# Softmax scaling split between ScalarE and VectorE, and the second 64-token score unit moved behind two other groups of products

## The chip, the cores and the metric

The kernel runs on one core of one Trainium2 chip. The metric is the device time of one execution in microseconds; the median of three runs counts. The engines of the core work in parallel, each through its own queue in order: TensorE (PE in the rows, its weight loads PEld), VectorE (DVE), ScalarE (ACT), GpSimd (POOL) and the queue that issues the transfers (SP).

## The reference

Two layers follow each other, for 8 batches of 576 tokens. The first is a causal retention over 8 heads of 64: `((q kᵀ / 8) * gamma_h^(i-j) for j <= i) v`. Its output, 512 wide, is the input `x` of the second, a mixture of 4 experts:

```python
logits = x @ w_gate                      # 4 experts, the best 2 chosen per token
w = softmax over the chosen 2
for e in range(4):
    a = softmax(causal((x @ wq[e]) @ (x @ wk[e]).T / 8))
    out += (e chosen) * w_e * (a @ (x @ wv[e]) @ wo[e])
```

What the change touches is the softmax `a`: the exponentials have to be divided by their sum and multiplied by the token's weight for the expert before they meet the values.

## The kernel before, in words

Tokens are cut into 36 tiles of 128 (9 for each pair of batches; the ninth holds the last 64 tokens of both), three tiles to a group, 12 groups. The main loop (line 514) runs over stages `j` = 0 to 14 and in each over three rounds `i` = 0, 1, 2. Round `i` of stage `j` does, in this order of issue:

- the retention of tile `n = 3j + i`: `qk(n+1)` (scores of the next tile), `old(n)` (product with the state), later `own(n)` (product inside the chunk) and `state(n+1)`;
- between `old` and `own`, the scores of the experts for one unit of group `j - 2` (`scores`, lines 330 to 382). A unit is one tile, or, for the ninth tile, two units of 64 tokens each ("tail" units). Both tail units fall into the third round. That happens in stages 4, 7, 10 and 13; I call the third rounds of stages 4, 7 and 10 the **tail rounds**. In stage 13 there is no retention left;
- the softmax of the unit: VectorE reads the scores from PSUM and finds the maxima (line 368, for tails 373), ScalarE exponentiates and sums (line 379), VectorE makes the reciprocal times the weight (lines 391 to 393) and scales (line 398). `normal(u)` holds lines 391 to 398;
- in between, as `work`, the projections of group `j - 1` (`pj` line 250 in one round, `pv` line 274 in the others) and the output product of group `j - 3` (`po` line 470);
- `split` (line 210 on ScalarE, 211 on GpSimd), which makes the two-part form of the retention's result.

After the three rounds the stage transposes the scaled weights on TensorE (`pt`, line 416), copies them out of PSUM on VectorE and ScalarE in turn (lines 420 and 422), works out the gate (lines 300 to 319), and multiplies with the values (`ys`, lines 442 to 449).

A unit's `p32` tile holds its pieces side by side: four experts for a whole unit, two pieces for a tail unit (expert pairs lie on the two halves of the partitions). A whole unit at place t = 0 to 3 of its batch has pieces 64 + 128t, 64 + 128t, 128 + 128t and 128 + 128t wide; a tail unit has two of 576. The second piece (`e` = 1) is scaled in two parts, the last 64 columns of it being written behind the first piece. So a whole unit has five scaling instructions (four at t = 0) and a tail unit three.

Engines, order and waits are fixed by the order of issue: each engine takes its instructions in program order, and an instruction waits only for the regions that it reads or writes. All PSUM tiles come from one pool of eight banks (`bank`, tag "b"); a bank is handed out again in the order in which the banks were given back, so each product on TensorE waits for the engine that empties the bank which is next in that order: `pv`, `pj` and `own` may wait for line 368 or 373, `own` for the copy of `qk` (line 144) or of `po` (line 473), `state` for the copy of `old` (line 169).

Of the kernel before, what the change touches and what calls it, by code (L numbers as in the profile page):

```python
# [11 lines left out]
AF = mybir.ActivationFunctionType  # L12
OP = mybir.AluOpType
# [18 lines left out]
def chunks(n):  # L32
    pair, i = divmod(n, 9)
    if i == 8:
        return [(2 * pair, 8), (2 * pair + 1, 8)]
    return [(2 * pair + i // 4, 2 * (i % 4)), (2 * pair + i // 4, 2 * (i % 4) + 1)]


def units(g):
    out = []  # L40
    for n in range(3 * g, 3 * g + 3):
        out += [(n, 0), (n, 1)] if n % 9 == 8 else [(n, None)]
    return out
# [3 lines left out]
def kernel(ctx: ExitStack, tc: tile.TileContext, xf, vkf, wraw, gi_d, con_d, out):  # L47
# [8 lines left out]
    act = nc.scalar.activation  # L56
    v = nc.vector
    gp = nc.gpsimd

    def bank(shape, name):  # L60
        return pool.tile(shape, F32, name=name, tag="b")
# [24 lines left out]
    def load(n, w):  # L86
        if n >= NT:
            return
        if w == 0:
            X[n] = x = ld.tile([128, 2, 4, 128], F32, name="x", tag="x")  # L90
            nc.sync.dma_start(x, xf[n])
        else:
            VK[n] = vk = ld.tile([128, 2, 2, 4, D], F32, name="vk", tag="vk", bufs=4)
            nc.sync.dma_start(vk, vkf[n])
# [6 lines left out]
    def decay(n, e=None):  # L101
        if n >= NT:
            return
        vv = VK[n][:, :, 0]
        k = chunks(n)[0][1]
        gm = gam[:, 8:9] if k == 8 else gam[:, k:k + 2]
        (e or gp).tensor_mul(vv, vv, gm.unsqueeze(3).to_broadcast([128, 2, 4, D]))  # L107

    def state(n):
        if n >= NT or n % 9 == 8:  # L110
            return
        vk = VK[n]
        ps = [bank([128, 2, 2, D], "st") for r in range(2)]
        for s in range(2):
            for u in range(2):
                for r in range(2):
                    for g in range(2):
                        h = 2 * g + u
                        mm(ps[r][HALF[g], s, u], vk[HALF[r], s, 1, h], vk[HALF[r], s, 0, h], start=True, stop=True)  # L119
        for s, (b, k) in enumerate(chunks(n)):  # L120
            last = k == 7
            S_[b, k] = w = sa.tile([128, 2, 2, D], F32, name="s7" if last else "s", tag="s7" if last else "s",
                                   bufs=3 if last else 4)
            for r in range(2):
                if k == 0:
                    v.tensor_copy(w[:, r], ps[r][:, s])
                else:
                    v.tensor_add(w[:, r], ps[r][:, s], S_[b, k - 1][:, r])
# [194 lines left out]
    def place(u):  # L323
        n, s = u
        if s is None:
            t = n % 9 % 4
            return t, SLOT[t], 4
        return 4, 3 + s, 2

    def scores(u):  # L330
        m, tail = u
        t, slot, n = place(u)
        g, l0 = m // 3, 128 * (m % 3)
        q, k = Q[g, "q"], K[g // 3]
        t0 = 128 * t
        ws = [t0 + 64, t0 + 64, t0 + 128, t0 + 128]
        if tail is None:
            kb = 512 * (m % 9 // 4)
            if t < 2:
                two = [bank([128, 2, t0 + 128], "ss") for z in range(2)]  # L340
                ps = [two[e % 2][:, e // 2, :ws[e]] for e in range(n)]
            else:
                ps = [bank([128, ws[e]], "ss") for e in range(n)]
            for s in range(2):
                for p in range(2):
                    for z in range(2):
                        e = 2 * s + z
                        mm(ps[e][HALF[p]], q[p][HALF[z], l0 + 64 * s:l0 + 64 * s + 64], k[p][HALF[z], kb:kb + ws[e]],  # L348
                           start=True, stop=True)
        else:  # L350
            kb = [slice(512 * tail, 512 * tail + 512), slice(1024 + 64 * tail, 1088 + 64 * tail)]
            ps = [[bank([128, 512 if j == 0 else 64], "ss") for j in range(2)] for z in range(2)]
            for j in range(2):
                for p in range(2):
                    for z in range(2):
                        mm(ps[z][j][HALF[p]], q[p][HALF[z], l0 + 64 * tail:l0 + 64 * tail + 64], k[p][HALF[z], kb[j]],
                           start=True, stop=True)
        p32 = sb.tile([128, PSZ[slot]], F32, name="p32", tag=f"p32{slot}")
        p32 = p32[:, :n * (t0 + 128)].rearrange("p (n w) -> p n w", n=n)
        sm = sb.tile([128, 2, E], F32, name="sm", tag="sm", bufs=6)  # L360
        nm = sb.tile([128, E], F32, name="nm", tag="nm", bufs=6)
        SS[u] = (p32, sm, ws)

        def soft():
            bias = []
            for e in range(n):
                if tail is None:
                    v.tensor_tensor_reduce(p32[:, e, :ws[e]], ps[e], mask[:, 576 - ws[e]:], -1.0, BIG, OP.add, OP.min,  # L368
                                           nm[:, e:e + 1])
                    bias.append(nm[:, e:e + 1])  # L370
                else:
                    for j, c in enumerate((slice(0, 512), slice(512, 576))):
                        v.tensor_tensor_reduce(p32[:, e, c], ps[e][j], mask[:, c],  # L373
                                               -1.0, nm[:, 2 * e:2 * e + 1] if j else BIG, OP.add, OP.min,
                                               nm[:, 2 * e + j:2 * e + j + 1])
                    bias.append(nm[:, 2 * e + 1:2 * e + 2])
            yield
            for e in range(n):
                act(p32[:, e, :ws[e]], p32[:, e, :ws[e]], AF.Exp, bias=bias[e], scale=-1.0, accum_out=sm[:, 0, e:e + 1])  # L379
                yield  # L380

        return soft()

    def normal(u):
        m, tail = u
        t, slot, n = place(u)
        t0 = 128 * t
        p32, sm, ws = SS[u]
        wt = WT[m // 3]
        rs = sm[:, 1, :n]  # L390
        v.tensor_scalar(sm[:, 0, :n], sm[:, 0, :n], 1e-9, None, op0=OP.add)
        v.reciprocal(rs, sm[:, 0, :n])
        v.tensor_mul(rs, rs, wt[:, m % 3].rearrange("p s z -> p (s z)") if tail is None else wt[:, 2, tail])  # L393
        for e in range(n):
            parts = [(e, 0, ws[e])] if e != 1 else [(1, 0, t0)] * (t > 0) + [(0, t0 + 64, 64)]
            for f_, c0, cw in parts:
                i0 = c0 if f_ == e else t0
                v.tensor_scalar(p32[:, f_, c0:c0 + cw], p32[:, e, i0:i0 + cw], rs[:, e:e + 1], None, op0=OP.mult)  # L398

    FLIP = [0]  # L400

# [75 lines left out]
    def run(*gs):  # L477
        for g in gs:
            for _ in g:
                pass  # L480
# [33 lines left out]
    for j in range(NG + 3):  # L514
        us = units(j - 2) if 0 <= j - 2 < NG else []
        for i in range(3):
            n = 3 * j + i
            if n < 2:
                decay(n + 1, v)
            if n != 2:  # L520
                qk(n + 1)
            old(n)
            work = stage(j, i)
            here = us[i:i + 1] if i < 2 else us[2:]
            soft = [scores(u) for u in here]
            for sc in soft:
                next(sc)
            own(n)
            if n == 2:
                qk(3)  # L530
            state(n + 1)
            load(n + 3, 0)
            load(n + 4, 1)
            if n == 0:
                fetch("o")
            scale(n, v if n < 3 else None)
            if 2 < n + 2 and i < 2:
                decay(n + 2)
            for u, sc in zip(here, soft):
                for _ in sc:  # L540
                    next(work, None)
                normal(u)
            split(n)
            if 0 < n + 1 < 5:
                table(n + 1)
            if i == 2:
                decay(n + 2)
            if n == 1:
                weights("k")
            if n == 2:  # L550
                weights("q", gp)
                weights("v")
            if n == 5:
                weights("o")
            run(work)
        for u in us:
            run(turn(u))
        if 0 <= j - 1 < NG:
            gate(j - 1)
        for u in us:  # L560
            values(u, u[0] == NT - 1)
# [56 lines left out]
```

## Time and profile before

| | |
|---|---|
| median of three runs | 477.23 us (476.7 to 477.42) |
| profiled execution, its own time | 473.82 us |
| its span, first to last instruction | 471.4 us |
| mean granted TensorE clock | 0.964 |
| PE busy | 434.9 us (92%) |
| DVE busy | 335.5 us (71%) |
| ACT busy | 260.3 us (55%) |
| POOL busy | 217.8 us (46%) |

The profile is of one execution; its own time is its span and 2.4 us around it, and it is 0.7% under the median of the runs. Times in the rows are microseconds from the start of the span. In a timeline row, the first number is the start, the second how long it (or the merged group, with x and its count) took, and brackets show how long the engine had been idle just before and which instruction ended that.

### The profile page before, as it was taken

How to read it: one execution, taken by the hardware profiler on the slowest of the kernel's cores; microseconds unless marked ns; L12 is line 12 of the kernel's file. 1: busy time of each engine (PE TensorE's matmuls, PEld its weight loads, DVE VectorE, ACT ScalarE, POOL GpSimd, SP SyncE). 2: the span in 40 equal slices, each digit the busy share in tenths (PEclk: the TensorE clock that was granted, in tenths of full speed). 3: DMA queues.
4: the chain of work that ended last, by engine and by line, in shares of the span. 5: the costliest groups of instructions: out<-in, count | busy, mean ns of one | idle time of the engine just before them, and what ended most of it. 6: DMA issues, size and time to landing. Idle time of an engine off the chain costs nothing.

```text
span 471.4 us, 18746 instructions
## 1 busy us (share of the span) xinstructions
PE 434.9 (92%) x7876; PEld 396.5 (84%) x7876; DVE 335.5 (71%) x1141; ACT 260.3 (55%) x762; POOL 217.8 (46%) x272
## 2 busy tenths in 40 slices
PE   6679888999989999999989999999999999999786
PEld 4578778889869998889969998889969999898476
DVE  2462777886898668886898678886898567665490
ACT  2545464664655564664665575664664466564552
POOL 4576573663653464563653365463653254202001
PEclk8679889999999999999999999999998999999979
DMA  8953432251351053242361063242250011010101
GB/s 279 405 204 117 155 99 83 92 182 68 110 186 46 26 198 119 90 159 92 93 202 48 1 214 125 91 160 91 92 203 3 3 36 36 1 68 2 68 1 69
DMA packets 18900, 50.90 MB, mean 108 GB/s; under 512 B 2304, under 2 KB 9088, under 8 KB 18816
## 3 DMA queue, kind: packets, MB, share of 16 engines
q1 hardware_dynamic: 18816, 49.71, 30.8%
q8 instruction: 62, 1.02, 0.9%
q14 instruction: 22, 0.18, 0.1%
HBM read 40.26 MB, written 9.44 MB: 105 GB/s over the span
## 4 chain that ended last, share of the span: by engine, by line
PE 77%; DVE 11%; ACT 4%; issue 4%; POOL 2%; DMA 1%; SPq 0%; ACTq 0%; POOLq 0%; DVEq 0%
PE pj L250 22%; PE pv L274 10%; PE pt L416 9%; PE po L470 7%; PE ys L442 6%; PE ss L348 5%; DVE p L398 5%; PE own L183 4%; PE qk L141 3%; PE st L119 3%; PE old L166 2%; DVE sm L393 2%; ACT p L379 2%; PE ys L449 2%; PE ys L446 2%
## 5 line engine op out<-in xcount | busy, mean ns | idle before, releaser
L379 ACT ACTIVATE p<-p,nm 128x128 f32<-128x128 f32 (+8 forms) x144 | 79.6, 554 | 41.8 <-DVE nm L368 27.2
L398 DVE TENSOR_SCALAR p<-p,sm 128x64 f32<-128x64 f32 (+8 forms) x176 | 81.6, 527 | 1.4
L460 POOL CAST yh<-y 128x256 fp32r<-128x256 f32 (+1 forms) x38 | 14.4, 379 | 124.5 <-ACT y L459 124.5
L147 POOL TENSOR_SCALAR_AFFINE_SELECT p<-p 64x512 f32<-64x512 f32 x72 | 49.1, 683 | 32.5 <-ACT p L144 29.9
L368 DVE CUSTOM_DVE_ANT_0 p<-ss,mask 128x128 f32<-128x128 f32 (+7 forms) x128 | 51.0, 453 | 17.2 <-PE ss L348 16.4
L200 POOL TENSOR_TENSOR x<-x,gi 128x512 f32<-128x512 f32 x29 | 37.4, 1290 | 47.7 <-DVE x L188 47.4
L211 POOL TENSOR_TENSOR xl<-x,xh 128x512 fp32r<-128x512 f32 x36 | 46.7, 1298 | 23.2 <-ACT xh L210 23.1
L420 DVE COPY pth<-pt 128x512 f32<-128x512 f32 (+2 forms) x52 | 31.3, 618 | 28.2 <-PE pt L416 27.8
L416 PE MATMUL pt<-con,p 128*128 128x128 f32 x360 | 43.8, 282 | 4.1 <-DVE nm L373 4.1
L416 PEld LDWEIGHTS pt<-con,p 128*128 128x128 f32 x360 | 42.5, 147 | 4.6 <-DVE nm L373 4.2
L183 PEld LDWEIGHTS own<-p,vk 64*64 64x64 f32 x1152 | 27.3, 144 | 21.9 <-issue 11.7
L183 PE MATMUL own<-p,vk 64*64 64x64 f32 x1152 | 28.8, 230 | 14.3 <-DVE nm L373 4.8
L442 PE MATMUL ys<-pth,vn 128*64 128x128 f32 (+1 forms) x640 | 39.2, 254 | 0.0
L348 PE MATMUL ss<-k,q 64*64 64x512 f32 (+7 forms) x512 | 38.9, 410 | 0.2
L107 POOL TENSOR_TENSOR vk<-vk,con 128x512 f32<-128x512 f32 x33 | 36.2, 1098 | 0.1
L422 ACT ACTIVATE pth<-pt 128x512 f32<-128x512 f32 (+2 forms) x52 | 27.3, 540 | 9.3 <-PE pt L416 9.3
L210 ACT ACTIVATE xh<-x 128x512 fp32r<-128x512 f32 x36 | 22.5, 626 | 17.3 <-POOL x L200 9.6
L473 ACT ACTIVATE ot<-po 128x384 f32<-128x384 f32 x48 | 23.4, 489 | 14.2 <-PE po L470 13.7
L442 PEld LDWEIGHTS ys<-pth,vn 128*64 128x64 f32 x640 | 29.0, 138 | 1.3 <-issue 1.2
L144 ACT ACTIVATE p<-qk 128x256 f32<-128x256 f32 x72 | 23.6, 379 | 11.9 <-PE qk L141 9.7
L141 PEld LDWEIGHTS qk<-x 64*64 64x64 f32 x1152 | 22.4, 145 | 9.2 <-issue 8.2
L119 PE MATMUL st<-vk 64*64 64x64 f32 x1024 | 26.1, 235 | 4.3 <-DVE vk L107 2.7
(93 smaller groups left out, 1051.3 us busy)
## 6 DMA issues: line engine op xcount, KB each, us to landing
x<-xf SPq DMA_DIRECT2D x36, 512.0 KB, 3.8
vk<-vkf SPq DMA_DIRECT2D x36, 512.0 KB, 4.7
out<-ot SPq DMA_DIRECT2D x48, 192.0 KB, 1.9
raw<-wraw SPq DMA_DIRECT2D x4, 512.0 KB, 8.8
gi<-gi SPq DMA_DIRECT2D x1, 256.0 KB, 8.2
con<-con SPq DMA_DIRECT2D x1, 110.0 KB, 3.3
mask<-con SPq DMA_DIRECT2D x1, 32.0 KB, 7.9
rg<-wraw SPq DMA_DIRECT2D x1, 8.0 KB, 8.8
```

The source lines that it names most:

```text
L119: mm(ps[r][HALF[g], s, u], vk[HALF[r], s, 1, h], vk[HALF[r], s, 0, h], start=True, stop=True)
L147: gp.affine_select(w, w, pattern=[[0, 8], [1, 64]], base=0, channel_multiplier=-1, compare_op=OP.is_ge, fill=0.0)
L183: mm(ps[r][HALF[u], g, i], vk[HALF[r], s, 0, 2 * g + u], p[HALF[r], g, s, u], start=True, stop=True)
L211: (e or gp).tensor_sub(xl[:, :, l0:l0 + 128], x32, f(xh[:, :, l0:l0 + 128]))
L250: mm(ps, ww[:, kc, p * 128:(p + 1) * 128], xx[:, kc, c], start=(i == 0), stop=(i == 11))
L274: mm(ps, xx[:, kc, l0:l0 + 128], ww[:, kc], start=(i == 0), stop=(i == 11))
L348: mm(ps[e][HALF[p]], q[p][HALF[z], l0 + 64 * s:l0 + 64 * s + 64], k[p][HALF[z], kb:kb + ws[e]], start=True, stop=True)
L368: v.tensor_tensor_reduce(p32[:, e, :ws[e]], ps[e], mask[:, 576 - ws[e]:], -1.0, BIG, OP.add, OP.min, nm[:, e:e + 1])
L379: act(p32[:, e, :ws[e]], p32[:, e, :ws[e]], AF.Exp, bias=bias[e], scale=-1.0, accum_out=sm[:, 0, e:e + 1])
L398: v.tensor_scalar(p32[:, f_, c0:c0 + cw], p32[:, e, i0:i0 + cw], rs[:, e:e + 1], None, op0=OP.mult)
L416: nc.tensor.transpose(pt[:, i], src, ident)
L442: mm(py[HALF[z], p], VN[n0 + j][:, e * D:(e + 1) * D], src, start=(j == 0), stop=False)
```

## The change

Two edits. In `normal`, the pieces with even `e` (the first and the third of a whole unit, the first of a tail unit) are scaled by a ScalarE copy with a per-token scale instead of a VectorE multiplication; the pieces with odd `e` stay where they are. In the main loop, only the first unit of a round has its scores issued ahead of `own` and `state`; a second one, which exists only in rounds with two tail units, has its scores and its VectorE maxima issued behind them.

```diff
             for f_, c0, cw in parts:
                 i0 = c0 if f_ == e else t0
-                v.tensor_scalar(p32[:, f_, c0:c0 + cw], p32[:, e, i0:i0 + cw], rs[:, e:e + 1], None, op0=OP.mult)
+                if e % 2 == 0:
+                    act(p32[:, f_, c0:c0 + cw], p32[:, e, i0:i0 + cw], AF.Copy, scale=rs[:, e:e + 1])
+                else:
+                    v.tensor_scalar(p32[:, f_, c0:c0 + cw], p32[:, e, i0:i0 + cw], rs[:, e:e + 1], None, op0=OP.mult)
...
-            soft = [scores(u) for u in here]
+            soft = [scores(u) for u in here[:1]]
             for sc in soft:
                 next(sc)
             own(n)
             if n == 2:
                 qk(3)
             state(n + 1)
+            for u in here[1:]:
+                soft.append(scores(u))
+                next(soft[-1])
```

## Rows read from the trace of the kernel before

**Rows 1.** The page: busy time, share of the span and instructions of each engine.
```profile
PE 434.9 (92%) x7876; PEld 396.5 (84%) x7876; DVE 335.5 (71%) x1141; ACT 260.3 (55%) x762; POOL 217.8 (46%) x272
```

**Rows 2.** The page: the chain that ended last, by engine.
```profile
PE 77%; DVE 11%; ACT 4%; issue 4%; POOL 2%; DMA 1%; SPq 0%; ACTq 0%; POOLq 0%; DVEq 0%
```

**Rows 3.** TensorE's waits: who waited for whom, total us, times, longest.
```profile
PE own L183 <- DVE nm L373: 4.8, 3, 1.6
PE pt L416 <- DVE nm L373: 4.1, 1, 4.1
PE own L183 <- DVE lg L289: 3.0, 3, 1.7
PE pj L250 <- DVE nm L368: 2.4, 3, 1.2
```

**Rows 4.** Timeline, VectorE, around the tail round of stage 7.
```profile
242.36 0.77 DVE L391 TENSOR_SCALAR sm<-sm 128x4 f32<-128x4 f32 x1 [0.25 <-ACT p L379]
243.38 1.22 DVE L393 TENSOR_TENSOR sm<-sm,wt 128x4 f32<-128x4 f32 x1
244.63 2.50 DVE L398 TENSOR_SCALAR p<-p,sm 128x448 f32<-128x448 f32 x5
```

**Rows 5.** The same stretch, GpSimd.
```profile
242.06 1.04 POOL L107 TENSOR_TENSOR vk<-vk,con 128x512 f32<-128x512 f32 x1
243.30 1.27 POOL L211 TENSOR_TENSOR xl<-x,xh 128x512 fp32r<-128x512 f32 x1 [0.20 <-ACT xh L210]
```

**Rows 6.** The same stretch, ScalarE.
```profile
242.14 0.20 ACT L379 ACTIVATION_READ_ACCUMULATOR p<-p,nm 128x1 f32 x1
242.60 0.63 ACT L210 ACTIVATE xh<-x 128x512 fp32r<-128x512 f32 x1
243.20 0.49 ACT L473 ACTIVATE ot<-po 128x384 f32<-128x384 f32 x1
243.82 0.66 ACT L144 ACTIVATE p<-qk 128x256 f32<-128x256 f32 x2
```

**Rows 7.** The same stretch, TensorE.
```profile
244.07 2.18 PE L356 MATMUL ss<-k,q 64*64 64x512 f32 x32
247.88 1.12 PE L183 MATMUL own<-p,vk 64*64 64x64 f32 x32 [1.63 <-DVE nm L373]
249.88 0.98 PE L250 MATMUL pj<-xh,whk 128*128 128x384 f32 x4
```

**Rows 8.** Timeline, VectorE, stage 13, where GpSimd is idle.
```profile
441.36 1.47 DVE L398 TENSOR_SCALAR p<-p,sm 128x320 f32<-128x320 f32 x5
447.62 1.74 DVE L398 TENSOR_SCALAR p<-p,sm 128x448 f32<-128x448 f32 x5
```

**Rows 9.** ScalarE by line and form: count, busy us, mean ns, idle before.
```profile
L379 ACT ACTIVATE p<-p,nm 128x512 f32<-128x512 f32 x16 | 11.4, 713 | 0.0
L379 ACT ACTIVATE p<-p,nm 128x128 f32<-128x128 f32 x16 | 6.2, 389 | 0.0
L99 ACT ACTIVATE gi<-gi,con 128x128 f32<-128x128 f32 x12 | 3.8, 386 | 0.0
```

**Rows 10.** Timeline, TensorE, second round of stage 2.
```profile
64.51 0.68 PE L183 MATMUL own<-p,vk 64*64 64x64 f32 x28 [1.72 <-DVE lg L289]
```

**Rows 11.** Timeline, ScalarE and TensorE, first and second round of stage 9.
```profile
308.90 0.49 ACT L473 ACTIVATE ot<-po 128x384 f32<-128x384 f32 x1 [0.56 <-PE po L470]
311.28 0.62 PE L183 MATMUL own<-p,vk 64*64 64x64 f32 x26 [0.89 <-DVE nm L368]
```

**Rows 12.** Timeline, ScalarE and TensorE, end of stage 13.
```profile
452.53 0.78 ACT L379 ACTIVATE p<-p,nm 128x576 f32<-128x576 f32 x1 [0.18 <-DVE nm L373]
454.36 1.82 ACT L422 ACTIVATE pth<-pt 128x512 f32<-128x512 f32 x4
457.49 0.66 PE L442 MATMUL ys<-pth,vn 128*64 128x128 f32 x8
```

**Rows 13.** Stretch, PE, PEld, DVE, ACT, POOL busy (count), granted clock, DMA share, GB/s.
```profile
356.00:358.00 2.00, 2.00 (x25) 1.93 (x15) 1.71 (x10) 1.34 (x4) 0.00 (x0) 0.56 0.03 8
```

## The prediction

> **What bounds the kernel now.** I read the page's busy times first, then the chain that ended last, then who waits for whom on TensorE, then the four engines side by side where TensorE waits. TensorE is busy 92% of the span [rows 1] and makes 77% of the last chain [rows 2]; VectorE has 11% of that chain and ScalarE 4%. So time is lost or won only where TensorE stands still. The list of its waits is short [rows 3]: 4.8 us in three pieces of 1.6 before `own`, for the maxima of the tail units; 3.0 us before `own`, for a VectorE copy behind the scaling; 2.4 us before `pj`; and 4.1 us once, at the end, before the transposes. All four end with VectorE, and in all of them VectorE is late because it was scaling the unit before. That is the most that the change can take away: some 14 us, less what takes its place.
>
> **The change, part by part.** *What moves.* 32 whole units give up two scalings each and 8 tail units one: 72 of 176.
>
> *VectorE's saving.* Where GpSimd is idle, the five scalings of a unit at t = 2 (1408 columns) took 1.47 us and at t = 3 (1920 columns) 1.74 us [rows 8]. The difference gives 0.53 ns a column, and what is left 0.15 us an instruction. First and third piece are 960 columns at t = 3, 704, 448 and 192 at t = 2, 1 and 0: saved 0.81, 0.67, 0.54, 0.40 us, and 0.46 for a tail. In all 8 x 2.42 + 8 x 0.46 = 23 us.
>
> *ScalarE's cost.* The trace has a scaled copy of another table, 128 wide: 12 in 3.8 us, 0.32 apart [rows 9]. The slope comes from exponentials 512 and 128 wide, 713 and 389 ns [rows 9]: 0.84 ns a column. So a unit costs ScalarE 1.23, 1.02, 0.80, 0.59 us (t = 3 to 0) and a tail 0.70, in all 35 us, on an engine with 211 us idle [rows 1]. Bounds from the rows: below, the columns alone (0.81 us at t = 3); above, full durations that don't overlap (1.37 us). I take 1.23, from the one row that is the same operation.
>
> *The new wait.* ScalarE takes its queue in order. Behind a unit's last exponential it now waits for lines 391 to 393. Behind that wait stand `xh` (line 210), the copies of `pv` and `po`, then those of `qk` and `old` of the next round, whose banks TensorE needs. What that wait costs: in stage 7 the last sum was ready at 242.34 [rows 6], line 391 ended at 243.13 and line 393 only at 244.60 [rows 4]. Both ended within 0.1 us of a GpSimd instruction: L107 at 243.10, L211 at 244.57 [rows 5]. But L211 needs `xh`, and `xh` will stand behind the scalings. So line 393, no longer beside L211, ends near 243.55, and the wait is about 1.2 us instead of 2.3; the VectorE scalings, 2.50 us beside GpSimd [rows 4], take 0.9 for three pieces.
>
> *The tail rounds (stages 4, 7, 10).* Worked through for stage 7. VectorE is free at 243.55 + 0.9 + some slack = 244.6 instead of 247.13 [rows 4], so it no longer is what is late. ScalarE: scalings 243.7 to 244.9, `xh` to 245.45, the `po` copy ends at 245.95 (before: 243.69), the `qk` copies at 246.25 and 246.5 (before: 244.48) [rows 6]. TensorE: the first tail's scores began at 244.07 and the two tails took 2.18 us together [rows 7]; the last bank of the first one is that of the `po` copy, so it finishes at 246.15, about 0.9 us late. `own` then needs the `qk` banks (246.55, just behind), ends near 246.95, `state` near 247.6, the second tail's scores, whose banks VectorE has emptied, near 248.7, and `pj` starts near 248.75 instead of 249.88 [rows 7]. Gain 1.1 us a round, 3.3 in all. The second edit does part of this: with it, `own` waits for `qk`'s banks and not for the first tail's maxima. Inside the round the exponentials of the second tail come later, but 8 us of `pj` hide that.
>
> *Stage 2.* The 1.72 us before `own` [rows 10] end when the last VectorE copy behind the scaling is done. Two waits of line 393 for GpSimd go, ScalarE adds its scalings ahead of that copy: I get 63.85 instead of 64.51, 0.7 us. The longest of the three `pj` waits, 1.2 us [rows 3], is in the third round of the same stage; the `qk` and `old` copies, then late, leave 0.5 us of gain. Together 1.2.
>
> *Where the wait only changes its name.* In stage 9 (and 3 and 6) `own` waited 0.89 us [rows 11]. The `po` copy that frees its first bank ended at 309.39 [rows 11]; behind 1.2 us of scalings and what they wait for it ends near 311.2, so `own` starts at the same 311.2. The same in the third rounds of stages 5, 8 and 11 to 0.1 us. I count these as 0.
>
> *The end (stage 13).* Here nothing covers. The order on ScalarE is: both exponentials of tail A, scaling of A, both of tail B, scaling of B, seven copies of transposes. The scaling of A waits for lines 391 to 393, which stand on VectorE behind the maxima of B. B's first exponential could start at 452.53 [rows 12], when the maximum of its first piece was there; the second's takes 0.9 more, 453.4. VectorE arrives 1.4 us earlier (0.67 + 0.81 less scaling in the two units before), so its maxima end at 452.05, lines 391 to 393 at 452.65, A is scaled by 453.4, so the first exponential of B starts at 453.4 instead of 452.53, and the copies start at 456.6 instead of 454.36 [rows 12]. The last transposes wait for the fifth of these, so `ys` starts near 459.1 instead of 457.49 [rows 12]: a loss of 1.6 us. TensorE, which stands idle 4.1 us ahead of the transposes today [rows 3], will then do so between them, so I add 0.4 for a lower clock.
>
> *Clock.* After the stall in stage 10 the granted clock was 0.56 for two microseconds and more [rows 13], the lower of its two levels, 1.2 GHz, for most of that time; 0.44 x 2 = 0.9 us. The stalls get shorter; I count half, 0.5 us.
>
> *Transfers.* Output transfers leave with the `po` copies, up to 2 us later, and the loads queue behind them on SP; they run two to three tiles ahead, so I count nothing. Were that cover gone, it would be these 2 us a round.
>
> **Sum.** -3.3 - 1.2 - 0.5 + 2.0 = -3.0 us: 470.8 against the profiled execution's 473.82. The same difference from the median of the runs: 474.2.
>
> **The rivals.**
> *A: ScalarE becomes what is late.* In 12 rounds (one each in stages 2, 3, 5, 6, 8 and 9, two each in 4, 7 and 10) I have TensorE start within 0.2 us of the moment when a ScalarE copy frees its bank. Each 0.1 us more per unit costs 1.2 us, so 0.25 us more than assumed uses up the gain. Price with 0.5 (the upper bound, 0.14, and a line 393 as late as before in a third of the rounds): 12 x 0.5 = 6, sum +3.0, 480.2. For it: the per-unit cost of 1.23 against 0.81 saved. Against it: ScalarE idles 211 us in all [rows 1], and where that idling stands ahead of a copy that has to wait for TensorE anyway, it catches up and the lateness doesn't add up from round to round. The Trainium skill, page "ScalarE: Activation LUTs", section "Rules for kernel authors", would keep a multiplication on VectorE because it is faster there per element. By that rule, 35 us bought with 23 would be a loss wherever ScalarE is on the chain; the rows agree on the prices, not on where the chain runs.
> *B: the wait changes its name in the tail rounds too.* Then -3.3 goes to 0: sum about +0.3, 477.5. For it: that is what I expect in stages 3, 5, 6, 8 and 9. Against it: in the tail rounds 2.5 us of VectorE lateness go.
> *C: more is won.* The stall at the end doesn't come, since ScalarE overlaps better than I count, and all clock drops go: -3.3 - 1.2 - 1.5 = -6.0, 471.2.
> *D: pieces of one `p32` tile on two engines wait for each other.* They touch different columns, so I don't expect it; it would act as A.
>
> **Chances.** My forecast 0.52, A with D 0.18, B 0.17, C 0.13. Two runs of this kernel can't be told apart below about 0.2%, 0.95 us. Faster by more: 0.62 (nearly all of the forecast, C, a little of B); same 0.17 (B); slower 0.21 (A, the rest). The range 470.6 to 478.2 holds C, forecast and B, and leaves out A's end. The forecast's own range is 472.2 to 476.2.
>
> **What would show it.** Tail rounds: no `own` wait for line 373, and `pj` about 1.1 us earlier after `qk`. Line 393 near 0.16 us instead of up to 1.22. New TensorE waits for ScalarE lines 473 and 144. In stage 13, exponentials of the second tail separated by a ScalarE wait for line 393, and `ys` later. I am wrong if TensorE's waits for ScalarE add up to more than 4 us, or if the tail rounds are no shorter.

## The result, and the profile after

The changed kernel took 471.62 us (median of 4 runs, 470.5 to 472.33) against 476.97 us of the kernel before on the same chip (4 runs): ratio 0.9885, 95% interval 0.9863 to 0.9907, or 5.4 us faster. Measured again beside the experiments it took 471.52 us against 476.07: ratio 0.9909 (0.9881 to 0.9936), 4.6 us. The forecast was 474.2, 3.0 us faster. The two profiled executions differ by 3.3 us (470.5 and 473.82) and their spans by 2.9 us (468.5 and 471.4).

The page after, against [rows 1, 2]: VectorE is busy 62.5 us less and has 4% of the last chain instead of 11%; ScalarE is busy 26 us more and has 7% of it instead of 4%.

```profile
PE 436.8 (93%) x7876; PEld 397.9 (85%) x7876; DVE 273.0 (58%) x1069; ACT 286.4 (61%) x834; POOL 216.1 (46%) x272
...
PE 79%; ACT 7%; DVE 4%; DMA 4%; issue 3%; POOL 1%; SPq 1%; ACTq 0%; POOLq 0%; DVEq 0%
```

TensorE's waits after (who waited for whom: total, times, longest), against [rows 3]. Lines behind 398 have moved by 3. The three waits of `own` for line 373 are gone; six shorter ones for the ScalarE copy of `po` (line 476) are new, and so is one of 2.1 us among the last transposes. One more for ScalarE stands under "issue": 2.11 us before `own` in stage 2, which ends just when the first `qk` copy does.

```profile
PE pt L419 <- DVE nm L373: 3.3, 1, 3.3
...
PE ss L356 <- ACT ot L476: 2.7, 3, 0.9
PE ss L348 <- ACT ot L476: 2.2, 3, 0.7
...
PE pt L419 <- DVE pth L423: 2.1, 1, 2.1
```

The tail round of stage 7 in the timeline after (start, duration), against [rows 4 to 7] and one more line of before, the GpSimd instructions beside which VectorE scaled there:

```profile
244.55 1.41 POOL L147 TENSOR_SCALAR_AFFINE_SELECT p<-p 64x512 f32<-64x512 f32 x2
```

After the change line 393 takes 0.16 us instead of 1.22, three scalings 0.98 instead of five in 2.50; L211 now starts 2.4 us behind L107, after the scalings. From `qk` to `pj` it is 246.65 - 240.95 = 5.70 us instead of 6.79.

```profile
240.95 0.69 PE L141 MATMUL qk<-x 64*64 64x64 f32 x32
243.96 0.34 PE L356 MATMUL ss<-k,q 64*64 64x64 f32 x6 [0.89 <-ACT ot L476]
246.65 0.97 PE L250 MATMUL pj<-xh,whk 128*128 128x384 f32 x4
...
240.22 1.01 DVE L391 TENSOR_SCALAR sm<-sm 128x4 f32<-128x4 f32 x1 [0.20 <-ACT p L379]
241.48 0.16 DVE L393 TENSOR_TENSOR sm<-sm,wt 128x4 f32<-128x4 f32 x1
241.67 0.98 DVE L401 TENSOR_SCALAR p<-p,sm 128x384 f32<-128x384 f32 x3
...
241.73 1.28 ACT L399 ACTIVATE p<-p,sm 128x448 f32<-128x448 f32 x2 [1.17 <-DVE sm L393]
243.44 0.47 ACT L476 ACTIVATE ot<-po 128x384 f32<-128x384 f32 x1
...
240.16 1.04 POOL L107 TENSOR_TENSOR vk<-vk,con 128x512 f32<-128x512 f32 x1
243.61 1.27 POOL L211 TENSOR_TENSOR xl<-x,xh 128x512 fp32r<-128x512 f32 x1 [2.40 <-ACT xh L210]
```

The end of stage 13 after, against [rows 12]: ScalarE waits 1.77 us for line 393 between the two tails' exponentials, as forecast, and the copies of transposes start late; TensorE stands 2.08 us between the transposes, and the first `ys` fall into the lower of its two clock levels (granted 0.51 in the row of the windows below).

```profile
447.07 0.78 ACT L399 ACTIVATE p<-p,sm 128x576 f32<-128x576 f32 x1 [1.77 <-DVE sm L393]
447.75 0.76 ACT L379 ACTIVATE p<-p,nm 128x576 f32<-128x576 f32 x1
...
450.73 2.80 ACT L425 ACTIVATE pth<-pt 128x512 f32<-128x512 f32 x6
...
451.30 2.55 PE L419 MATMUL pt<-con,p 128*128 128x128 f32 x14 [2.08 <-DVE pth L423]
453.77 1.12 PE L445 MATMUL ys<-pth,vn 128*64 128x128 f32 x8
```

Two stretches of the windows after (columns as in [rows 13]): behind the tail round of stage 10 the clock now stays at 1.00, where it was 0.56 before; at the end it is low under the first `ys`, where before it was at 1.00 again from 456 us on, ahead of `ys` at 457.49 [rows 12].

```profile
352.00:354.00 2.00, 2.00 (x23) 1.75 (x15) 1.85 (x8) 0.49 (x2) 1.40 (x2) 1.00 0.57 213
...
452.00:455.00 3.00, 3.00 (x24) 2.67 (x24) 1.93 (x4) 1.81 (x5) 0.00 (x0) 0.51 0.00 0
```

### The profile page after: what moved, and what is told of

Its sections match the earlier page's. It is cut to its first block, busy times and chain, and to the rows that moved or that the text cites. A ratio compares the mean times of both kernels' runs of the same rounds, so it can differ in the third digit from the quotient of the medians.

```text
span 468.5 us, 18762 instructions
## 1 busy us (share of the span) xinstructions
PE 436.8 (93%) x7876; PEld 397.9 (85%) x7876; DVE 273.0 (58%) x1069; ACT 286.4 (61%) x834; POOL 216.1 (46%) x272
## 4 chain that ended last, share of the span: by engine, by line
PE 79%; ACT 7%; DVE 4%; DMA 4%; issue 3%; POOL 1%; SPq 1%; ACTq 0%; POOLq 0%; DVEq 0%
PE pj L250 22%; PE pv L274 11%; PE pt L419 8%; PE po L473 8%; PE ss L348 7%; PE ys L445 6%; PE own L183 4%; DMA x<-xf 4%; PE qk L141 4%; PE st L119 3%; PE old L166 2%; ACT p L379 2%; PE ys L452 2%; DVE sm L391 2%; PE ys L449 2%
## 5 line engine op out<-in xcount | busy, mean ns | idle before, releaser
L211 POOL TENSOR_TENSOR xl<-x,xh 128x512 fp32r<-128x512 f32 x36 | 46.1, 1280 | 89.3 <-ACT xh L210 89.3
L399 ACT ACTIVATE p<-p,sm 128x64 f32<-128x64 f32 (+4 forms) x72 | 37.0, 556 | 42.0 <-DVE sm L393 42.0
L147 POOL TENSOR_SCALAR_AFFINE_SELECT p<-p 64x512 f32<-64x512 f32 x72 | 48.7, 676 | 20.3 <-ACT p L144 17.7
L419 PE MATMUL pt<-con,p 128*128 128x128 f32 x360 | 45.1, 287 | 5.4 <-DVE nm L373 3.3
L348 PE MATMUL ss<-k,q 64*64 64x64 f32 (+7 forms) x512 | 41.7, 409 | 2.2 <-ACT ot L476 2.2
L183 PEld LDWEIGHTS own<-p,vk 64*64 64x64 f32 x1152 | 28.5, 142 | 13.4 <-issue 10.4
L183 PE MATMUL own<-p,vk 64*64 64x64 f32 x1152 | 30.4, 229 | 6.6 <-ACT xh L210 2.8
L107 POOL TENSOR_TENSOR vk<-vk,con 128x512 f32<-128x512 f32 x33 | 35.4, 1074 | 0.3 <-DMA vk<-vkf 0.3
L391 DVE TENSOR_SCALAR sm<-sm 128x4 f32<-128x4 f32 (+1 forms) x40 | 15.5, 388 | 30.6 <-ACT p L379 30.0
L401 DVE TENSOR_SCALAR p<-p,sm 128x64 f32<-128x64 f32 (+4 forms) x104 | 29.1, 333 | 1.4
```

The costliest lines, as they stand in the source:

```text
L147: gp.affine_select(w, w, pattern=[[0, 8], [1, 64]], base=0, channel_multiplier=-1, compare_op=OP.is_ge, fill=0.0)
L183: mm(ps[r][HALF[u], g, i], vk[HALF[r], s, 0, 2 * g + u], p[HALF[r], g, s, u], start=True, stop=True)
L211: (e or gp).tensor_sub(xl[:, :, l0:l0 + 128], x32, f(xh[:, :, l0:l0 + 128]))
L419: nc.tensor.transpose(pt[:, i], src, ident)
```

## The experiments

**How they are compared.** In each trace a round is timed from the first `qk` matmul of one tile to that of the next. The table gives these lengths for the kernel before and, for the others, the difference from it, in us. "2nd" is the sum of the second rounds of stages 3, 6 and 9; "end" runs from the last `qk` to the first `ys` of stage 13; "low" counts the pieces of low granted clock between 40 and 400 us (each 1.7 us of clock time, read from the windows by 1 us). The tail rounds and the second rounds of the table agree between two traces of one kernel to 0.1 us wherever no such piece falls into them; those of stage 2, which are not in it, differ by over 1 us. The tail round of stage 10 held a piece before, worth 27.35 - 25.84 = 1.5 us.

| kernel | ratio to before (95%) | stage 4 tail | stage 7 tail | stage 10 tail | 2nd | end | low |
|---|---|---|---|---|---|---|---|
| before | 1 | 25.84 | 25.84 | 27.35 | 22.22 | 72.37 | 3 |
| changed | 0.9885 (0.9863 to 0.9907) | -1.12 | -1.12 | -2.61 | -0.36 | +2.03 | 1 |
| e1, before again | 0.9993 (0.9966 to 1.0019) | 0.00 | +1.53 | -1.50 | -0.06 | +0.21 | 4 |
| e10, changed again | 0.9909 (0.9881 to 0.9936) | -1.14 | -1.12 | -2.62 | -0.32 | +2.64 | 1 |
| e2, scaling alone | 0.9891 (0.9858 to 0.9925) | -1.19 | -1.17 | -2.69 | -0.34 | +2.32 | 1 |
| e3, order alone | 0.9953 (0.9929 to 0.9977) | +1.26 | -0.28 | -1.79 | +0.04 | -0.05 | 4 |
| e4, last tails on VectorE | 0.9837 (0.9799 to 0.9875) | -1.10 | -1.12 | -2.62 | -0.38 | -1.40 | 1 |
| e5, before, split late | 0.9847 (0.9814 to 0.988) | +0.29 | +0.30 | +0.03 | -2.54 | -0.08 | 3 |
| e6, changed, split late | 0.9906 (0.9875 to 0.9937) | -1.09 | -1.11 | -2.64 | -0.41 | +2.46 | 0 |
| e9, e4 and split late | 0.9801 (0.977 to 0.9832) | -1.10 | -1.11 | -2.64 | -0.39 | -1.53 | 1 |
| e12, one unit back | 1.0024 (1.0 to 1.0049) | -0.28 | -0.28 | -1.80 | -0.35 | +1.97 | 2 |
| e7, all on ScalarE | 1.041 (1.0378 to 1.0442) | +0.24 | +1.83 | +0.30 | +5.13 | +3.96 | 4 |
| e11, one unit, split late | 0.9752 (0.9725 to 0.978) | -1.17 | -1.17 | -2.67 | -2.49 | -0.59 | 1 |

**e1: the kernel before, unchanged.**

> The kernel before, unchanged, to see how its span spreads from run to run. The profiled pair differs by 2.9 us of span (471.4 to 468.5), the medians by 5.35 us. Theory 1 (the rest is clock): the runs near the median hold more stretches at the lower granted clock than the profiled one; then the spans here run from about 471 to 475 us, the longer ones with a lower mean clock than 0.964, and the time of a run is its span and about 2.4 us. Theory 2 (the rest is a stall that one execution in several lacks): spans differ by over 2 us at the same mean clock. Theory 3 (the profiled run was drawn from another chip or day): all spans here lie within 0.5 us of each other.

Twelve runs took 472.05 to 477.38 us, spans 470.3 to 475.3, the longer ones mostly with a mean clock of 0.957 to 0.960, the shorter ones 0.967 to 0.971. Its trace (474.8 us) is 3.4 us longer than that of before: 1.4 us by 40 us, where the low clock lasts to 36 us instead of 32 and runs into `pj`; 2.4 more by the end of stage 2, with pieces at 49, 66 and 76 us (before: at 55 and 66); +1.53 in the tail round of stage 7, -1.50 in that of stage 10. So the piece stood in stage 7 this time and not in stage 10. Here it is, right behind the 1.63 us wait of `own` that this kernel has in all three tail rounds [rows 7]:

```profile
251.56 1.12 PE L183 MATMUL own<-p,vk 64*64 64x64 f32 x32 [1.63 <-DVE nm L373]
```

```profile
252.00:254.00 2.00, 1.94 (x62) 1.74 (x63) 1.71 (x9) 1.64 (x5) 0.00 (x0) 1.00 0.22 47
254.00:256.00 2.00, 2.00 (x9) 2.00 (x8) 1.85 (x9) 0.85 (x2) 0.17 (x1) 0.50 0.56 215
```

Theory 1 fits: the two traces differ where their stretches of low clock differ, and of the twelve runs the longer ones mostly have the lower mean clock.

**e10: the changed kernel, unchanged.**

> The changed kernel, unchanged, on the chip of the other three of this call. So far its four runs spread over 1.8 us and those of the kernel before over 5 us, and in the traces TensorE's clock goes low in pieces that cost 1.7 us each (the kernel before: 1 to 4 of them between stage 2 and stage 11, the changed one none in the one trace). Theory (the changed kernel's shorter stalls set off fewer of these pieces): its runs again spread less than 2.5 us, median 4 to 6 us under the kernel before, and its trace shows at most one such piece between 70 and 435 us. Rival (chance of the profile): as many pieces and as wide a spread as before, median 3 us under.

Six runs, 470.12 to 471.9 us, a spread of 1.8; in the same minutes before spread over 5.4 (472.74 to 478.15). One piece of low clock between 40 and 400 us, at 62 us, none in a tail round. As the theory said.

**e2: the scaling alone.**

```diff
-            soft = [scores(u) for u in here[:1]]
+            soft = [scores(u) for u in here]
...
-            for u in here[1:]:
-                soft.append(scores(u))
-                next(soft[-1])
```

> Only the first edit: first and third piece scaled by ScalarE, all scores ahead of own. My theory: the first edit makes VectorE free 2.5 us earlier in a tail round, but own still stands behind the first tail's maxima, and these behind a ScalarE copy of po that is now late, so a tail round gains about 0.6 us instead of 1.1; stage 2 gains 1.2, the clock drop of stage 10 goes (about 1.5), the end loses 2.8: -1.8 - 1.2 - 1.5 + 2.8 = -1.7 us against the kernel before. Rival (the two edits are independent and the first does everything): the same time as the changed kernel, -5. Rival (ScalarE is late, the order edit hides it): slower than before by 1 to 3 us.

469.87 us, within its interval the same as the changed kernel. Its tail rounds gain 1.17 to 1.19 us without the clock piece, no less than with both edits. My 0.6 was wrong: with VectorE early, the maxima of the first tail follow the scores at once and `own` waits for nothing, in the old order too. The first rival was right.

```profile
240.12 0.70 PE L141 MATMUL qk<-x 64*64 64x64 f32 x32
...
243.14 1.63 PE L356 MATMUL ss<-k,q 64*64 64x64 f32 x16 [0.90 <-ACT ot L476]
244.43 0.28 PE L183 MATMUL own<-p,vk 64*64 64x64 f32 x2
...
245.74 0.97 PE L250 MATMUL pj<-xh,whk 128*128 128x384 f32 x4
```

**e3: the order alone.** The second tail's scores behind `own` and `state`, as in the change; all scaling on VectorE.

> Only the second edit: the second tail's scores behind own and state, all scaling on VectorE. My theory: the stall moves from own to the second tail's scores and pj, since VectorE's scaling (2.5 us) still stands ahead of the maxima and of the additions that empty own's and state's banks: 0.3 to 0.5 us gained per tail round, nothing in stage 2 and at the end: -0.9 to -1.5 us. Rival (the order is the whole gain of the tail rounds): -1.1 x 3 and the clock drop, -4.8 us. Rival (the order only moves the wait): 0.

472.65 us, 0.5% faster by the ratio, or 2.2 us. Apart from the clock pieces the tail rounds gain 0.28 each (25.84 to 25.56 in stage 7), 0.8 in all; where the rest of the 2.2 lies its trace, with a span 0.6 us longer than that of before, does not show. In the tail round the wait of 1.6 us now stands before the second tail's scores, as expected, since VectorE is still busy with five scalings.

```profile
250.68 1.83 PE L356 MATMUL ss<-k,q 64*64 64x512 f32 x16 [1.57 <-DVE nm L373]
...
247.53 2.48 DVE L398 TENSOR_SCALAR p<-p,sm 128x448 f32<-128x448 f32 x5
```

**e4: the last two tails back on VectorE.**

```diff
-                if e % 2 == 0:
+                if e % 2 == 0 and (tail is None or m < NT - 1):
```

> The changed kernel with the two tail units of the very last token group scaled by VectorE alone, as before. In stage 13 of the changed profile the exponentials of the second tail stand behind a ScalarE scaling that waits 1.77 us for line 393, and the output weights' last stage starts 2.8 us late against the stages ahead of it. My theory: that wait is the whole loss, so the span gets shorter by about 2.0 to 2.8 us than the changed kernel's, ys follows the first exponential of stage 13 by 16.8 us again instead of 18.7, and the line 399 scalings of the tails in stage 13 are gone. Rival (the loss comes from the copies of transposes on ScalarE or from the clock after the stall): less than 0.7 us shorter.

467.33 us, 2.3 to 3.4 us under the changed kernel by the ratios. From the last `qk` to the first `ys` it is 74.40 - 70.97 = 3.4 us less than in the changed kernel's trace, to the end of the span 4.3 us, more than expected: the end is now also 1.4 us shorter than before, and the whole units ahead of the tails, still halved on VectorE, would explain it (1.3 of it lies ahead of the transposes). All four exponentials follow the maxima 1.05 us apart again:

```profile
444.84 0.78 ACT L379 ACTIVATE p<-p,nm 128x576 f32<-128x576 f32 x1 [0.18 <-DVE nm L373]
445.89 0.78 ACT L379 ACTIVATE p<-p,nm 128x576 f32<-128x576 f32 x1 [0.18 <-DVE nm L373]
...
450.77 0.66 PE L445 MATMUL ys<-pth,vn 128*64 128x128 f32 x8
```

**e5: before, with `split` late.** Nothing is scaled by ScalarE.

```diff
-            split(n)
             if 0 < n + 1 < 5:
...
             run(work)
+            split(n)
```

> The kernel before with one step moved and no scaling moved: split(n), whose ScalarE copy xh releases GpSimd's line 211, stands behind the rest of the round's projections instead of ahead of them. Theory (VectorE was late because lines 393 and 398 stood beside line 211, not for the number of its scalings): line 393 in the tail rounds takes about 0.2 us instead of 1.22 and the five scalings 1.5 to 1.8 us instead of 2.50, VectorE is free about 1.7 us earlier, the po copy comes 0.6 us earlier; a tail round gains 1 us or more and one clock piece or more goes: 4 to 6 us faster than before. Rival (the number of VectorE scalings is the cause): under 1 us.

468.36 us, 7.7 us faster than before, more than the 4 to 6 expected, and not where I expected it. In its trace, whose span is 5.8 us shorter, the second rounds of stages 3, 6 and 9 gain 0.8 us each, those of 4, 7 and 10 0.3, the third rounds of 5 and 8 0.6; 1.4 us are gained by the end of stage 2, and the tail rounds lose 0.3. In the second round of stage 9 line 211 no longer stands beside line 393, which takes 0.16 us instead of 1.00, and `own` runs in one piece where it waited 0.89 us [rows 11]. In a tail round lines 211 and 147 fall right onto the scalings, which take 3.60 us instead of 2.50, and `own` waits 1.92:

```profile
239.47 0.16 DVE L393 TENSOR_TENSOR sm<-sm,wt 128x4 f32<-128x4 f32 x1
239.67 3.60 DVE L398 TENSOR_SCALAR p<-p,sm 128x448 f32<-128x448 f32 x5
...
240.19 1.40 POOL L211 TENSOR_TENSOR xl<-x,xh 128x512 fp32r<-128x512 f32 x1 [0.99 <-ACT xh L210]
241.54 1.45 POOL L147 TENSOR_SCALAR_AFFINE_SELECT p<-p 64x512 f32<-64x512 f32 x2
...
244.02 1.12 PE L183 MATMUL own<-p,vk 64*64 64x64 f32 x32 [1.92 <-DVE nm L373]
...
305.61 0.96 PE L183 MATMUL own<-p,vk 64*64 64x64 f32 x30
```

So the mechanism (VectorE is held up beside GpSimd) is shown, in both directions; that a late `split` alone would help the tail rounds is refuted.

**e6: the changed kernel with `split` late.** The same move of `split` as in e5.

> The changed kernel with split(n) behind the rest of the round's projections. In the changed profile TensorE waits six times, 4.9 us in all, before the tails' scores for the po copy, ahead of which ScalarE made xh (0.6 us). Theory (ScalarE's order is what is left of the wait): 0.5 us less in each of the six, 2 to 3 us faster than the changed kernel. Rival (the wait goes on to own, for the qk copies behind the po copy): under 0.7 us. Rival (xh later makes the next stage or GpSimd late): slower.

471.01 us, the same as the changed kernel. The six waits for the `po` copy shrink, but in the tail rounds TensorE then waits for the `qk` copies behind it (three times, 1.6 us in all), and the second rounds of stages 3, 6 and 9 gain nothing either; those of stages 4, 7 and 10 gain 0.3 to 0.5 us on the changed kernel's, and the third rounds of 3, 6 and 9 lose 0.3 to 0.6. The first rival was right.

```profile
PE own L183 <- ACT p L144: 1.6, 3, 0.5
```

**e9: both, e4 and e6.**

> The changed kernel with split(n) late and the last two tail units scaled by VectorE alone. Theory (the two are independent): the sum of both, 2 to 3 us from the order and 3 to 4 from the end, that is 464 to 466 us, 10 to 12 under the kernel before. Rival (both only spare clock pieces, which are spared once): about 467, as with the end alone.

466.28 us; the end gains as in e4, the late `split` nothing clear of the noise (ratio 0.9801 against e4's 0.9837, with intervals that overlap). The rival is nearer.

**e12: one unit back.** The unit ahead of each tail round is scaled by VectorE alone.

```diff
-                if e % 2 == 0:
+                if e % 2 == 0 and m % 9 != 7:
```

> The changed kernel, with the unit that stands just ahead of each tail round (m % 9 == 7) scaled by VectorE alone; the other 28 whole units and the tails as in the changed kernel. Theory (the tail rounds' gain is that one unit's, since its scaling stands ahead of the tails' maxima): the third rounds of stages 4, 7 and 10 get 0.8 to 1.1 us longer again, with TensorE waiting for VectorE line 373 there, and a clock piece of 1.5 us comes back in about one of the three: 3 to 5 us slower than the changed kernel; stage 2 and the rounds between do not move. Rival (the gain is spread over all units): under 1.5 us slower. Rival (VectorE's lateness was line 211's doing, and line 211 now comes early again behind xh): the rounds get as long as before, with line 393 at 1.2 us again.

475.32 us, 0.2% slower than before: 4 of 36 tiles cost the whole gain. The tail rounds lose 0.84, 0.84 and 0.81 us against the changed kernel, and TensorE waits three times, 4.7 us in all, for line 373. These 2.5 us are what its trace shows of the theory; its span is 4.2 us longer than the changed kernel's, the ratios differ by 5.5 to 6.6 us, no clock piece fell into its tail rounds, and where the rest lies was not settled. The last rival was right at the same time: with no scaling ahead of `xh`, line 211 is early again, and line 393 long.

```profile
243.31 0.99 DVE L393 TENSOR_TENSOR sm<-sm,wt 128x4 f32<-128x4 f32 x1
244.34 2.48 DVE L401 TENSOR_SCALAR p<-p,sm 128x448 f32<-128x448 f32 x5
...
243.00 1.28 POOL L211 TENSOR_TENSOR xl<-x,xh 128x512 fp32r<-128x512 f32 x1
```

**e7: all pieces on ScalarE.**

```diff
-                if e % 2 == 0:
+                if True:
```

> The changed kernel with all pieces on ScalarE, that is 176 scalings instead of 72. It doubles what rival A of the prediction fears. Theory (ScalarE is the late one wherever TensorE now waits for the po copy): each of the six such waits of the changed kernel grows by the second half of a unit's scaling, about 1.4 us at t = 3, and the end by another 2 to 3: 8 to 11 us slower than the changed kernel, 4 to 6 slower than before. Rival (ScalarE's 182 idle us take it up): within 2 us of the changed kernel.

494.37 us, 20 us slower than before, where I had expected 4 to 6. The waits for the `po` copy double in number (12 against 6) and length, and each costs the round in which it falls; I had counted six. All second rounds of stages 3 to 10 but two lose 1.2 to 2.6 us, the 2.6 with a clock piece in it, and the third rounds of 5 and 8 lose 1.1 each.

```profile
PE ss L348 <- ACT ot L476: 10.3, 8, 2.1
PE ss L356 <- ACT ot L476: 7.3, 4, 2.3
```

```profile
253.92 2.64 ACT L399 ACTIVATE p<-p,sm 128x448 f32<-128x448 f32 x5 [1.19 <-DVE sm L393]
```

**e11: one unit on ScalarE, `split` late.** From the kernel before: `split` as in e5, and

```diff
+                if e % 2 == 0 and m % 9 == 7:
+                    act(p32[:, f_, c0:c0 + cw], p32[:, e, i0:i0 + cw], AF.Copy, scale=rs[:, e:e + 1])
+                else:
```

> The kernel before with split(n) behind the round's projections, and with first and third piece on ScalarE for the units with m % 9 == 7 alone. Theory (two separate causes: line 211 beside VectorE's lines 393 and 398 in the second rounds, VectorE's own scaling ahead of the tails' maxima in the third rounds of stages 4, 7 and 10): the second rounds keep the 0.6 to 0.9 us that the late split gained, the tail rounds gain 1.1 each and their clock pieces, the end is no later than before: 463 to 465 us, 11 to 13 under the kernel before and faster than every other version. Rival (ScalarE's scaling ahead of the po copy eats the late split's gain here too): 467 to 469, as the late split alone.

462.27 us against 474.3, ratio 0.9752: the fastest version, 2.5% under before. The second rounds keep e5's gain, the tail rounds get the change's, the end is 0.6 us shorter than before. The two causes are separate.

```profile
235.96 0.69 PE L141 MATMUL qk<-x 64*64 64x64 f32 x32
...
241.58 0.97 PE L250 MATMUL pj<-xh,whk 128*128 128x384 f32 x4
...
236.50 0.16 DVE L393 TENSOR_TENSOR sm<-sm,wt 128x4 f32<-128x4 f32 x1
236.69 0.98 DVE L401 TENSOR_SCALAR p<-p,sm 128x384 f32<-128x384 f32 x3
```

## Why the prediction was right, and where it was not

The direction was right, and so were the tail rounds and the end. The measured 471.62 us lies 0.6 us under the forecast's own range (472.2 to 476.2). The profiled pair: tail rounds -3.36, clock piece of stage 10 -1.5, up to the end of stage 2 -1.05, end +2.85, the rest +0.2, together -2.9. The terms of the sum in turn:

- **Tail rounds, -1.1 each: right** (-1.12, -1.12, and -1.11 in stage 10 without its clock piece), and along the forecast path: line 393 at 0.16 us, first tail held 0.89 us by the `po` copy, `pj` 1.09 us earlier. Two details were wrong. "The second edit does part of this": it does not; beside the first edit it is worth nothing (e2), alone 0.28 us (e3). And most of the gain, 0.8 of 1.1, belongs to one unit in nine (e12), the one whose scaling stands ahead of the tails' maxima.
- **Stage 2, -1.2: right in size, by luck.** In the profiled pair `own` of the second round starts 2.86 us behind `qk` instead of 3.80 [rows 10], 0.9 less where I had 0.7. But the third round, where I had 0.5 less, is 0.3 longer, since `own` there waits 2.11 us for the copy of `qk`; and 0.5 us are the lower clock that only the trace of before has, at 66 us. Nor does the 0.9 stand: the same distance is 3.97 us in e10 and 3.95 in e12, both with the changed code in this stage, and 2.08 in e3, where VectorE does all the scaling. What the change is worth here was not settled. The changed kernel, then e12:

```profile
63.64 0.68 PE L183 MATMUL own<-p,vk 64*64 64x64 f32 x28 [0.78 <-ACT p L144]
...
70.34 0.94 PE L183 MATMUL own<-p,vk 64*64 64x64 f32 x30 [2.11 <-issue]
```

```profile
60.58 0.69 PE L141 MATMUL qk<-x 64*64 64x64 f32 x32
...
64.53 0.68 PE L183 MATMUL own<-p,vk 64*64 64x64 f32 x28 [1.88 <-ACT p L144]
```

- **The wait that changes its name, 0: right.** The second rounds of stages 3, 6 and 9 together are 0.36 us shorter; those of stages 4, 7 and 10, which I had left out, 0.7 longer.
- **The end, +2.0: right cause, too small.** `ys` comes 2.03 us later after the last `qk` where I had 1.6, and the output 0.8 later again, the first `ys` being at the lower clock, where I had 0.4. e4 shows that the two tail units' ScalarE scaling is the cause.
- **Clock, -0.5: the step that failed.** "The stalls get shorter; I count half, 0.5 us." In these traces a piece of low clock is there whole or not at all, and costs the tail round into which it falls 1.2 to 1.6 us; the one of stage 10 alone made 1.5 us in the profiled pair. In the five traces whose tail rounds keep a stall of 1.5 to 1.9 us (before, e1, e3, e5, e12) it fell into 4 of 15 tail rounds, in stage 4, 7 or 10; in the seven with that unit's scaling on ScalarE and stalls of 0.9 us or less (changed, e10, e2, e4, e6, e9, e11) into none of 21. That it goes with the stall and not with where the scaling is done, e7 speaks for: all on ScalarE, six stalls of 2.1 to 2.3 us, and a piece behind three of them. Between 40 and 80 us the five have 2 or 3 pieces, the seven 0 or 1.
- **What the sum left out: the medians gain more than the profiled pair.** The profiled execution of before had 3 pieces in all, e1's 4, and e1's span of 474.8 is nearer to the median run. The difference between -2.9 in the profiled pair and -4.6 to -5.4 in the medians, 1.7 to 2.5 us, has the size of one or two such pieces. The single executions fit this. Six of each kernel had a mean clock of 0.967, with spans of 471.8 us on average before and 469.6 after, 2.2 us apart; over all executions beside the experiments and after the change (63 and 10) it is 473.0 and 469.4, 3.6 apart. In which stages the median run has its pieces was not settled.
- **Transfers, 0: right,** as far as TensorE's waits show: the three for loads of `x` in the changed kernel, 1.4 us in all, lie in the first 26 us.

A measure that I gave for being wrong fired without my being wrong: TensorE's new waits for ScalarE add up to 7.8 us (4.9 for copies of `po`, 2.9 in stage 2 for those of `qk`), over 4. Three of the six `po` waits only replace VectorE waits of the same length in the second rounds, which my bound did not allow for. Of the rivals, A is real at twice the dose (e7) and not at this one. B is what happens in the second rounds only. C named nearly the measured time, 471.2, with half of its reasons: the clock pieces go, but the stall at the end does come; its 1.5 us for the clock had no working, and that it equals the piece of stage 10 is luck.

The prediction had all four of TensorE's waits end with a VectorE that was late "because it was scaling the unit before". That was part of it, and the list left out another 2.8 us that `own` waited for line 368 (one of its three waits is in [rows 11]). VectorE's busy time fell by 62.5 us where its own columns account for 23. The rest is time that it had spent held beside GpSimd. In the trace of before, 55 of the 176 scalings ran beside a GpSimd instruction and took 31 us more than the others of the same widths, and line 393 took 12 us more in 15 of its 40 times; in the changed one none of 104 and 2 of 40 did. The same five scalings took 1.74 us with GpSimd idle [rows 8], 2.50 beside L147 [rows 4], 3.60 beside L211 and L147 (e5). The Trainium skill, page "SBUF — State Buffer", section "Who interferes with whom", has a rule for this: a VectorE instruction with two SBUF inputs contends with a GpSimd instruction that reads SBUF, and one in a two-port mode with any; whichever issues first keeps the other out for its whole instruction. For line 393, which has two SBUF inputs, these traces agree: 0.16 us alone, it takes 0.99 to 1.22 when L211 started first, and ends with it. In which mode the scalings ran no trace shows.

The rule of the Trainium skill that the prediction weighed (page "ScalarE: Activation LUTs", section "Rules for kernel authors": multiply on VectorE) holds for the instruction and not for the kernel here: two pieces cost ScalarE 1.28 us and spare VectorE 1.74 - 0.98 = 0.76 [rows 8], yet the tail rounds get 1.1 us shorter; with all pieces on ScalarE the kernel is 20 us slower (e7).

## What to carry to other kernels

Before moving work off an engine that is late, see what makes it late: here GpSimd instructions beside VectorE cost it 1.06 us in line 393 and 0.76 in the scalings of a tail round, and moving one of them a little later in the queue (e5) won more than moving 72 scalings, though not in the tail rounds. Then move only the instructions that stand ahead of what the engine that bounds the time waits for: with `split` late, one unit in nine was enough (e11), and the two units of the last tile alone cost 4 us at the end of the kernel (e4), where nothing covers. And where a clock can drop behind a stall, compare medians and several traces, since a piece of low clock may be in one trace and not in the next.

## What was not expected of the hardware

The granted clock of a kernel that did not change fell in another tail round from one execution to the next (at 356 us in one trace, 254 in the other), behind the same 1.63 us stall, at a cost of 1.5 us each time; behind stalls of 0.9 us or less it fell in none of 21 tail rounds.
